# Pooling k and v in the load for six of eight batches, with the schedule laid out anew for it

## The chip, the cores and the metric

The kernel runs on one core of a Trainium2 chip. The metric is the time of one execution on the device, in microseconds (us). Before the change the median of three runs is 214.1 us (213.88 to 214.9).

The engines have short names here as in the profile: PE multiplies matrices (PEld is its loading of the stationary operand), DVE and ACT work elementwise, POOL (GpSimd) issues the loads and sets up constants, SP issues the stores. Each engine executes its own instructions in order; semaphores order the engines among each other.

## The reference

Two parts, one after the other, over 8 batches of 576 tokens:

```python
# attention: q, k, v are (8 batches, 8 heads, 576, 64)
k_p = k.reshape(B, H, 72, 8, D).mean(axis=3)      # 8 neighbours pooled
v_p = v.reshape(B, H, 72, 8, D).mean(axis=3)
scores = scale * np.matmul(q, k_p.transpose(0, 1, 3, 2))
attn = softmax(scores)
x = np.matmul(attn, v_p)                          # -> (8, 576, 512)
# gated FFN: w_in 512x1024, conv_w 3x1024, w_out 1024x512
h = np.maximum(x @ w_in, 0.0)
conv_out = sum(conv_w[k] * shifted(h, k - 1) for k in range(3))   # along the tokens
gate = 1.0 / (1.0 + np.exp(-conv_out))
out = (h * gate) @ w_out
```

All inputs and the output are float32 in memory; the kernel computes in bfloat16 with float32 sums.

## The kernel before

The work of a batch b runs through these stages (line numbers are those of the profile):

- Loads, all issued by POOL, with a cast to bfloat16 on the way: k into `k_b` (L291 for batch 0, L297 for the others), q into `q_b` (L279), v into `v_b` (L321). Each of these tiles exists twice, for even and odd batches, so a load for batch b+2 waits until batch b's data have been read. A row of `k_b` or `v_b` holds the 8 neighbours to be pooled side by side, 8 x 64 = 512 values; there are 576 such rows for each tensor and batch (96 partitions x 6 for k, 72 x 8 for v).
- Pooling on DVE, by halving three times. For k: `kp1` = left half + right half of the row (L406; L402 in two parts for batch 0), `kp2` of that (L414), `ksum` of that (L419). For v: `vp1` (L453), `vp2` (L459) and `vaug` (L465).
- Transposes on PE: `ksum` (L432, copied out to `kTz` at L438 by DVE or ACT) and q (L477, in three groups, copied out to `qT` at L483).
- Scores on PE (L502) per head, exp on ACT (L514), the product with `vaug` on PE (L534, per tile of 128 tokens, "av"), the softmax's division on DVE (L543, L547, into `xx`), the transpose on PE (L561) and a copy to `xT` (L567, DVE or ACT).
- mm1 on PE (L606; L583 in parts for batch 0) and relu on ACT (L612, L590) into `hT`.
- The convolution, per block of 128 features. Blocks that are listed in `off` multiply the three shifted copies on DVE (L632) or ACT (L630), add them on DVE (L638) and take tanh on ACT (L643); the other blocks do it on PE with diagonal matrices `dw` (L680, tanh at L687). The gate is finished on DVE (L660, L666, into `gT`).
- mm2 on PE for pairs of batches (L706), copied to `osb` (L733, L721) and stored by SP (L738, L726).

The order of all this is not written out. A planner inside the kernel (class `Planner`) is given every step with the engines that can do it, an assumed duration, what it reads and writes, and a priority. It plays the steps through once before anything is emitted: on each engine the step that can start first goes next, ties within 0.02 us going to the lower priority number; it also decides between DVE and ACT where a step may run on either, and which of five PSUM slots (three of two banks, two of one) a step gets. The instructions are then emitted in that order, and on the chip each engine keeps it, whatever the real times are. Loads are steps of POOL in this plan, with an assumed time to land. Where the plan sees PE idle in the first 60 us it puts in matmuls of zeros (L254).

The dictionary `PARAMS` holds the numbers that steer the plan: for each batch the priorities of k pooling and transposes (`k`), of q (`q`), of v pooling (`v`), of the scores (`s`, with `ds` from head to head), of av, of the convolution, of mm2 for each group of output tiles; `ld0` and `ps0` for the loads and scores of batch 0; `off` as above; and `acc`, for each batch how many of the three halvings are left to the load. Before the change `acc` is 0 throughout. The code for other values is there already:

Of the kernel before, what the change touches and what calls it, by code (L numbers as in the profile page):

```python
# [13 lines left out]


PARAMS = {
    "off": [(3, 4, 5, 7), (1, 2, 3, 6, 7), (0, 1, 2, 3, 5, 7), (0, 1, 3, 4, 5, 6, 7), (0, 1, 2, 3, 4, 5, 6, 7), (0, 1,
        2, 3, 5, 6, 7), (0, 1, 2, 3, 4, 5, 6, 7), (0, 1, 2, 3, 4, 5, 7)],
    "acc": [0, 0, 0, 0, 0, 0, 0, 0],
    "ld0": [24.66, 0.21, 24.87, 29.62],  # L20
    "ps0": [-13.48, 7.04, 25.02],
    "k": [-8.55, -8.2, -0.72, -12.54, -4.52, -6.0, -8.43, 3.78],
    "q": [-6.36, -3.15, -9.81, 0.97, -2.95, -1.4, -1.88, -9.39],
    "v": [13.91, 4.49, 21.33, 8.22, 1.58, 4.69, 0.09, 45.0],
    "s": [7.35, -3.51, -9.19, -0.57, -3.02, -1.5, -0.0, -6.38],
    "ds": [3.55, 0.71, 1.7, 0.82, 1.36, 0.51, 0.22, -0.62],
    "av": [3.86, 7.06, 3.44, -6.76, -3.51, 4.03, 3.95, -21.37],
    "conv": [3.75, 4.11, 3.3, 3.75, 6.31, 1.04, -10.08, 10.39],
    "mm2": [22.45, 26.52, 17.23, 19.82, 22.07, 21.94, 16.92, 25.3, 19.34, 26.01, 18.91, 22.24, 14.48, 13.2, 21.88,
        3.71, 17.65, 13.25, 17.78, 18.72],  # L30
}


# [793 lines left out]
```

## Time and profile before

The profiled execution:

| what | value |
|---|---|
| time of the profiled execution | 214.1 us |
| its span in the profile | 212.3 us |
| granted PE clock | 1.00 in every stretch |
| PE matmuls, L606 (mm1) | 448, 61.6 us busy |
| PE matmuls, L706 (mm2, 512 columns) | 263 recorded, 63.8 us busy |
| DVE in all | 427 instructions, 185.9 us |
| of it k and v pooling (L402 to L465) | 51 instructions, 35.4 us |
| ACT in all | 301 instructions, 171.1 us |
| DMA, loads (queue 0) | 15648 packets, 16.26 MB written |
| DMA, stores (queue 1) | 5124 packets, 9.45 MB |
| last load issued | 104.2 us (q of batch 7) |

Span is the time from the first to the last recorded instruction of the core; the execution's own time has some 1.8 us around it. A group of instructions is given by line, engine, operation, output and input, and how often it occurs; then the time in which at least one of them ran, the mean duration of one in ns, and the idle time of the engine just before them with what ended it. Matmuls overlap in their pipeline, so the mean duration of one is more than the distance from one to the next.

### The profile page before, as it was taken

The numbers are of one execution on the slowest core, as the hardware profiler recorded it, in microseconds if no ns is written. First come the engines' busy times: TensorE is split into PE (matmuls) and PEld (weight loads), VectorE is DVE, ScalarE is ACT, GpSimd is POOL, SyncE is SP. The second block draws the span as 40 slices with busy tenths as digits, with TensorE's granted clock in tenths as the row PEclk, the third lists the DMA queues.
The fourth block names the chain that finished last, engine by engine and source line by source line (L and its number), as shares of the span: only waits on it lengthen the run. The fifth ranks groups of instructions, "written<-read, shape, count | busy, mean of one in ns | idle before, by whom it ended". The sixth has DMA issues, their size and how long they took to land.

```text
span 212.3 us, 4744 instructions
## 1 busy us (share of the span) xinstructions
PE 200.2 (94%) x1888; PEld 143.7 (68%) x1905; DVE 185.9 (88%) x427; ACT 171.1 (81%) x301; POOL 34.7 (16%) x68
## 2 busy tenths in 40 slices
PE   8998999799999999999999999899999999999983
PEld 8987776687676876577865876566675766655432
DVE  1468699999999999999999999999999998999700
ACT  2074589879996998579999899999799999997632
POOL 7947962011211111020100000000000000000000
PEclk9999999999999999999999999999999999999999
DMA  5999999999999996879442200032020203005125
GB/s 79 157 187 203 205 187 213 196 198 204 183 165 233 178 157 148 121 142 221 67 100 100 99 3 0 3 150 81 21 99 0 102 0 148 3 0 196 66 88 198
DMA packets 20794, 26.02 MB, mean 123 GB/s; under 512 B 2444, under 2 KB 15268, under 8 KB 20772
## 3 DMA queue, kind: packets, MB, share of 16 engines
q0 software_dynamic: 15648, 16.26, 49.6%
q1 hardware_dynamic: 5124, 9.45, 11.9%
q8 instruction: 15, 0.25, 0.5%
q14 instruction: 7, 0.06, 0.1%
HBM read 32.52 MB, written 9.44 MB: 198 GB/s over the span
## 4 chain that ended last, share of the span: by engine, by line
DVE 51%; PE 28%; ACT 3%; issue 3%; ACTq 0%
PE psfB L706 14%; DVE cv L638 10%; DVE cv L632 10%; PE psfA L606 9%; DVE xx L547 7%; DVE gT L666 5%; DVE tg L660 3%; DVE qT L483 3%; DVE vp L453 3%; DVE kp L406 2%; DVE kTz L438 1%; DVE vp L459 1%; PE psfA L502 1%; DVE xT L567 1%; DVE rr L543 1%
## 5 line engine op out<-in xcount | busy, mean ns | idle before, releaser
L706 PE MATMUL psfB<-w_out,gT 128*128 128x512 bf16 (+1 forms) x279 | 65.7, 373 | 2.1 <-ACT osb L733 0.8
L606 PE MATMUL psfA<-xT,w_in 128*128 128x288 bf16 x448 | 61.6, 286 | 0.7 <-ACT hT L612 0.5
L606 PEld LDWEIGHTS <-w_in 128*128 128x128 bf16 x448 | 43.2, 98 | 12.6 <-issue 1.2
L706 PEld LDWEIGHTS <-gT 128*128 128x128 bf16 x296 | 28.1, 98 | 29.4 <-issue 2.1
L638 DVE TENSOR_TENSOR cv<-cv 128x1152 bf16<-128x1152 bf16 (+1 forms) x60 | 40.2, 669 | 0.1
L632 DVE TENSOR_SCALAR cv<-hT,cw 128x576 bf16<-128x576 bf16 x118 | 38.6, 366 | 1.8 <-ACT hT L590 1.1
L514 ACT ACTIVATE attnT<-psfA 72x576 bf16<-72x576 f32 (+3 forms) x70 | 38.4, 604 | 0.3
L612 ACT ACTIVATE hT<-psfA 128x576 bf16<-128x576 f32 x56 | 35.8, 652 | 3.1 <-PE psfA L606 2.9
L643 ACT ACTIVATE tg<-cv 128x1152 bf16<-128x1152 bf16 (+1 forms) x30 | 31.3, 1043 | 5.1 <-DVE cv L638 4.8
L630 ACT ACTIVATE cv<-hT,cw 128x576 bf16<-128x576 bf16 x38 | 28.9, 781 | 0.4
L547 DVE TENSOR_TENSOR xx<-psfA,rr 128x512 bf16<-128x512 f32 x40 | 26.5, 684 | 0.1
L733 ACT COPY osb<-psfB 128x512 f32<-128x512 f32 x32 | 18.5, 583 | 9.6 <-PE psfB L706 6.8
L666 DVE TENSOR_TENSOR gT<-tg,hT 128x1152 bf16<-128x1152 bf16 x32 | 24.0, 750 | 0.2
L502 PE MATMUL psfA<-qT,kTz 128*72 128x288 bf16 (+3 forms) x140 | 23.4, 269 | 0.3
L502 PEld LDWEIGHTS <-kTz 128*72 128x72 bf16 x160 | 16.1, 113 | 4.5 <-issue 1.0
L561 PEld LDWEIGHTS <-xx 128*128 128x128 bf16 x160 | 10.4, 97 | 8.8 <-DVE xx L547 6.1
L660 DVE TENSOR_SCALAR tg<-tg 128x1152 bf16<-128x1152 bf16 x32 | 14.4, 451 | 2.1 <-ACT tg L687 1.1
L534 PE MATMUL psfA<-vaug,attnT 72*128 72x65 bf16 x320 | 14.7, 194 | 1.2 <-ACT hT L590 0.6
L534 PEld LDWEIGHTS <-attnT 72*128 72x128 bf16 x320 | 12.9, 98 | 2.4 <-ACT attnT L514 0.9
L254 PEld LDWEIGHTS <-zero 128*128 128x128 bf16 x192 | 13.4, 109 | 1.0 <-DVE zero L341 1.0
L561 PE MATMUL psbB<-perm,xx 128*128 128x128 bf16 x120 | 11.7, 220 | 1.8 <-DVE xx L547 1.5
L254 PE MATMUL pswA<-zero 128*128 128x128 bf16 x160 | 12.0, 244 | 1.0 <-DVE zero L341 1.0
(65 smaller groups left out, 211.4 us busy)
## 6 DMA issues: line engine op xcount, KB each, us to landing
out_dram<-osb SPq DMA_DIRECT2D x15, 512.0 KB, 2.8
k_b<-in_k_dram POOLq DMA_DIRECT2D x7, 576.0 KB, 11.9
q_b<-in_q_dram POOLq DMA_DIRECT2D x7, 576.0 KB, 11.2
v_b<-in_v_dram POOLq DMA_DIRECT2D x7, 576.0 KB, 10.8
out_dram<-osb SPq DMA_DIRECT2D x5, 256.0 KB, 2.1
w_in<-in_moe_w_in_dram POOLq DMA_DIRECT2D x4, 256.0 KB, 10.3
w_out<-in_moe_w_out_dram POOLq DMA_DIRECT2D x2, 512.0 KB, 17.1
k_b<-in_k_dram POOLq DMA_DIRECT2D x2, 288.0 KB, 4.8
```

The lines of the kernel that those rows point to most:

```text
L502: nc.tensor.matmul(out=t[:, par, :], lhsT=kTz[m][:, par, h * Sp:(h + 1) * Sp], rhs=qT[m][:, 2 * c0:2 * c1, h * A:(h + 1) * A], start=True, ...
L514: nc.scalar.activation(out=attnT[m][:, h, :].rearrange("p (c i x) -> p i c x", i=2, x=32)[:, :, c0:c1, :], in_=view().rearrange("p i (c x) ...
L534: nc.tensor.matmul(out=a[:, h // 4, c:c + D + 1], lhsT=attnT[m][:, h, u0:u0 + 128], rhs=vaug[m][:, h, :], start=True, stop=True)
L547: nc.vector.tensor_tensor(out=xx[i3].rearrange("p (g h e) -> p g h e", g=2, h=4), in0=av_view()[:, :, :, 0:D], in1=rr[i3].rearrange("p (g ...
L606: nc.tensor.matmul(out=t[:, i, 0:HC], lhsT=w_in[:, c, f * P:(f + 1) * P], rhs=xT[m][:, c, i * HC:(i + 1) * HC], start=(c == 0), stop=(c == ...
L612: nc.scalar.activation(out=hT[m][:, f, 2:S + 2].rearrange("p (i x) -> p i x", i=2), in_=slot(key)[:, :, 0:HC], func=ACT.Relu, scale=0.5)
L630: nc.scalar.activation(out=cv[y][:, kk, z, :], in_=src, func=ACT.Copy, scale=s)
L632: nc.vector.tensor_scalar(out=cv[y][:, kk, z, :], in0=src, scalar1=s, scalar2=None, op0=OP.mult)
L638: nc.vector.tensor_tensor(out=cv[y][:, 1, 0:n, :], in0=cv[y][:, 1, 0:n, :], in1=cv[y][:, kk, 0:n, :], op=OP.add)
L643: nc.scalar.activation(out=tg[i3][:, f0 % 2:f0 % 2 + n, :], in_=cv[y][:, 1, 0:n, :], func=ACT.Tanh, scale=0.5)
L666: nc.vector.tensor_tensor(out=gT[(b // 2) % 2][:, fs[0]:fs[0] + 2, o:o + S], in0=tg[i3], in1=hT[m][:, fs[0]:fs[0] + 2, 2:S + 2], op=OP.mult)
L706: nc.tensor.matmul(out=a[:, 0, 0:cols.stop - cols.start], lhsT=g[:, c, t * P:(t + 1) * P], rhs=w_out[:, c, cols], start=(c == 0), stop=(c ...
```

## The change

Only `PARAMS` changes:

```diff
-    "off": [(3, 4, 5, 7), (1, 2, 3, 6, 7), ... (0, 1, 2, 3, 4, 5, 7)],
-    "acc": [0, 0, 0, 0, 0, 0, 0, 0],
-    "ld0": [24.66, 0.21, 24.87, 29.62],
-    "ps0": [-13.48, 7.04, 25.02],
-    "k": [-8.55, -8.2, -0.72, -12.54, -4.52, -6.0, -8.43, 3.78],
-    "q": [-6.36, -3.15, -9.81, 0.97, -2.95, -1.4, -1.88, -9.39],
-    "v": [13.91, 4.49, 21.33, 8.22, 1.58, 4.69, 0.09, 45.0],
-    "s": [7.35, -3.51, -9.19, -0.57, -3.02, -1.5, -0.0, -6.38],
...
+    "off": [(3, 4, 6, 7), (1, 2, 3, 6, 7), ... (0, 1, 2, 3, 4, 5, 6)],
+    "acc": [0, 0, 1, 1, 2, 2, 2, 2],
+    "ld0": [12.84, 6.71, 2.4, 13.31],
+    "ps0": [4.03, 25.62, 23.84],
+    "k": [-1.85, -9.12, 6.44, -3.93, -3.45, -1.33, -20.69, 4.21],
+    "q": [1.98, -27.92, -7.96, -2.38, -0.51, -6.81, -1.77, -5.87],
+    "v": [0.33, -18.28, 26.25, 0.55, 0.78, 4.94, 13.58, 25.95],
+    "s": [-13.2, -14.96, 5.26, -2.65, -3.09, -0.39, -0.96, -3.9],
...
```

`ds`, `av`, `conv` and `mm2` get new numbers in the same way. In `off` only batch 0 (block 6 in place of 5) and batch 7 (block 6 in place of 7) differ.

`acc` leads to code that did not run before. For a batch with `acc` = 1 the load of k is split in two, each bringing half of the 512 values of a row: the first writes the half row, the second adds its half to what is there (L307). With `acc` = 2 there are four loads of a quarter row. v is treated in the same way:

```python
n = 2 ** PARAMS["acc"][b]
w = 512 // n
for i in range(n):
    kw = {} if i == 0 else {"accum_op": OP.add}
    nc.gpsimd.dma_start(out=dst[:, :, 0:w], in_=src[:, :, i * w:(i + 1) * w], **kw)
```

Each adding load reads and writes what the one before it wrote, so POOL issues it only after the one before it has landed. For `acc` = 1 the steps `kp1` and `vp1` on DVE fall away, for `acc` = 2 also `kp2` and `vp2`; the next step reads `k_b` or `v_b` directly, so the tile stays in use until then.

The new priorities give new orders on all engines. In POOL's order the loads now stand as follows, from the first load for batch 2 on (k4.1 is the second load of batch 4's k, and so on):

```
k2.0 q2 v2.0 k3.0 q3 v3.0 k2.1 q4 v2.1 k3.1 q5 v3.1
k4.0 q6 v4.0 k5.0 k4.1 v5.0 v4.1 k5.1 q7
k4.2 v5.1 v4.2 k5.2 k4.3 v5.2 v4.3 k5.3
k6.0 v5.3 v6.0 k6.1 k7.0 v6.1 v7.0 k6.2 k7.1 v6.2 v7.1 k6.3 k7.2 v6.3 v7.2 k7.3 v7.3
```

Of these k6.0 waits for `ksum` of batch 4, v6.0 and v7.0 for `vaug` of batches 4 and 5, k7.0 for `ksum` of batch 5, q6 and q7 for the q transposes of batches 4 and 5. On PE the k transposes of batches 2 to 5 stand later than before among the other matmuls, those of batches 2 and 3 after the whole mm1 of batch 1.

## The prediction

> **What bounds the kernel now.** I read the page's engine shares and slices first, then a table of busy time by stage, then the chain of waits in order of time, then the DMA part.
>
> ```profile
> span 212.3 us, 4744 instructions
> PE 200.2 (94%) x1888; PEld 143.7 (68%) x1905; DVE 185.9 (88%) x427; ACT 171.1 (81%) x301; POOL 34.7 (16%) x68
> DMA  5999999999999996879442200032020203005125
> ```
>
> PE, DVE and ACT are all nearly full, and DMA is full for the first 80 us and nearly empty after 115 us. The stages tell more (window, its length, then busy us and instructions of each engine):
>
> ```profile
> 0.00:46.00 46.00, 41.89 (x531) 35.52 (x532) 33.40 (x77) 27.21 (x67) 26.91 (x57) 1.00 1.17 180
> 46.00:78.00 32.00, 30.98 (x301) 23.09 (x302) 31.45 (x69) 29.63 (x51) 4.68 (x7) 1.00 1.10 194
> 78.00:119.00 41.00, 39.47 (x365) 27.28 (x368) 40.91 (x96) 34.83 (x60) 3.15 (x5) 1.00 0.62 119
> 119.00:155.00 36.00, 35.04 (x319) 24.75 (x321) 36.00 (x85) 34.12 (x55) 0.00 (x0) 1.00 0.14 53
> 155.00:212.30 57.30, 52.77 (x386) 33.02 (x388) 44.14 (x105) 45.33 (x72) 0.00 (x0) 1.00 0.22 83
> ```
>
> From 46 to 155 us DVE never rests (108.4 of 109 us) and the chain of waits runs over DVE in most of this stretch; from 157 us it runs over PE. But PE is idle only 1.02 + 1.53 + 0.96 = 3.5 us between 46 and 155. Busy time of pipelined matmuls covers short gaps, so I also count by spacing, which the chain gives where PE runs without a break:
>
> ```profile
> 162.94 1.73 PE psfB L706 x8
> 171.30 0.52 PE psfA L534 x16
> 177.32 5.88 PE psfA L606 x48
> ```
>
> That is 216 ns for 512 columns, 33 ns for 65 and 122 ns for 288; the 128-column transposes stand 56 ns apart, the 96-column ones 42. The PE stream, priced so, needs 102.7 us from the q transposes of batch 2 (L477, start 46.7 us) to the k transposes of batch 7 (L432, start 155.3 us), which took 108.6: 5.9 us of PE gaps. So a faster DVE can win 3.5 to 5.9 us there and no more.
>
> **The change, part by part.** Pooling taken off DVE:
>
> ```profile
> L453 DVE TENSOR_TENSOR vp<-v_b 72x2048 bf16<-72x2048 bf16 x7 | 8.5, 1215 | 0.0
> L406 DVE TENSOR_TENSOR kp<-k_b 96x1536 bf16<-96x1536 bf16 x7 | 6.7, 962 | 0.8 <-DMA k_b<-in_k_dram 0.8
> L459 DVE TENSOR_TENSOR vp<-vp 72x1024 bf16<-72x1024 bf16 x7 | 4.8, 680 | 0.0
> L414 DVE TENSOR_TENSOR kp<-kp 96x768 bf16<-96x768 bf16 x8 | 4.4, 547 | 0.0
> ```
>
> L406 and L453 go for six batches, L414 and L459 for four: 6 x (0.962 + 1.215) + 4 x (0.547 + 0.680) = 18.0 us. The new order also moves work between DVE and ACT: DVE takes one kTz copy (0.45), one qT copy (0.42), seven whole and two half xT copies (7 x 0.417 + 2 x 0.286) and two osb copies (2 x 0.686), 5.7 us, and gives seven products (L632, 0.366) to ACT, -2.6. DVE: -18.0 + 5.7 - 2.6 = -14.9 us. ACT gives up 7.3 us for these copies and takes 7 x 0.781 = 5.5: -1.8 us. On PE the matmuls are the same but for three warm-up ones (0.17 us); the lists "off" change in which filters they hold, not in how many (52 before and after), so this edit costs nothing. Worth on the path: of the 3.5 to 5.9 us of gaps, ACT (near 9/10 full) and the order keep some; I take **-3**, bounds 0 and -5.9. After 155 us nothing is taken: there PE, not DVE, sets the end.
>
> Reordering of batch 0's loads: the same two k loads go first; q then stands behind the identity (0.22 + 0.29 us) and w_in starts about 0.3 us later than 7.97. DVE waits 1.0 us in all for those first k loads and 1.6 for v. I take 0, bounds -1 and +1.
>
> Loads: a pooled load reads 1/2 (batches 2, 3) or 1/4 (4 to 7) of each row and adds it to the destination, and each waits for the one before it to land. For k and for v alike the nine issues of before (two halves of batch 0, one each of batches 1 to 7) become 2 + 1 + 2 x 2 + 4 x 4 = 23, so 28 more in all. While POOL stands in such a wait, all loads behind it in its order wait too, q included. On POOL each costs what these do, 0.74 to 0.87 us: 22 us, on an engine that is 84% idle; nothing. What counts is the DMA queue itself, which works in order:
>
> ```profile
> q0 software_dynamic: 15648, 16.26, 49.6%
> k_b<-in_k_dram POOLq DMA_DIRECT2D x7, 576.0 KB, 11.9
> v_b<-in_v_dram POOLq DMA_DIRECT2D x7, 576.0 KB, 10.8
> ```
>
> A k or v load is 576 packets whatever its width. Single packets in the trace took 98 ns at 1024 B written (k, v before) and 60 ns at 512 B (w_in). A line through both gives 41 ns at 256 B, so an unaccumulated quarter load keeps 16 engines 576 x 41 / 16 = 1.48 us; four of them are 5.9 us against 3.5 us for the one load they replace. The trace has no accumulating packet. It reads 512 B of source and 256 B of destination; by bytes read (512 B at 41 ns, 1024 B at 60) that is 50.5 ns, 1.82 us a load. Lower bound 41 ns; upper bound two packets' worth, 82 ns, 2.95 us. I take 50.5, nearest to the two rows. Batches 2 and 3 (60 ns x 2 x 576 against 98 x 576) add 0.8 us each to a queue that is full until 80 us, but their pooled sums stand late in the new order (below), so I price them at nothing; without that cover it would be 3.2 us.
>
> Where does it become late? I placed the changed streams on the clock by the spacing count plus the lag of count behind clock that the kernel before shows (12.4 us at its batch-4 k transposes, 13.6 at batch 5, 14.4 at batch 6, 15.1 at the q transposes of batch 6). Batch 2's and 3's k sums then stand at 62 and 66 us, more than 10 us behind their loads. But POOL's issue of q for batch 7 waits for the last six q transposes of batch 5 (count 65.9, so 78.5 us), and behind it in POOL's order stand 20 quarter loads up to the last one of batch 6's k. The sum that needs it (ksum, L419) and the six transposes behind it on PE stand at count 104.3, so 119.4 us. Between: 41 us. Work for the DMA engines in it: q7, 128 packets x 361 ns / 16 = 2.9 us; 4 first and 16 accumulating loads, 5.9 + 16 x 1.82 = 35.0; some 4.5 output stores of 256 packets x 85 ns / 16, 6.1; 1.8 us from issue to first packet and from last packet to semaphore (1.5 us seen). Sum 45.8: **4.8 us late**. At 41 ns it is 40.3, just in time; at 82 ns 63.9, 23 us late. These sums let all 16 engines work alike; a v load took 5.3 us from first to last packet for 3.6 us of mean engine time, so the ten v loads can be half as long again: 10 x 1.75 x 0.5 = 8.7 at most. I add a third of it, **+2.9**. Behind the late sum wait DVE (products of batch 4) and, in order, PE (mm1 and mm2), so the wait is paid by both.
>
> A rule of the Trainium skill speaks against the change more strongly: SBUF — State Buffer, in "SBUF: two separate sides", says that DVE's two-port modes lock GpSimd out while it writes the descriptors of its DMAs, and gives 620 ns growing to 3100. The row disagrees: POOL's k and v issues took 740 to 798 and 752 to 869 ns with DVE 40.9/41 busy, and 704 to 822 at 1.3 us with DVE idle. By the rule a chain of four would be some 10 us longer; by the row, nothing.
> DMA: Bandwidth & Descriptors (Specifications) says that transfers below 512 B lose line rate to a read-modify-write; no run here shows packets of 256 B on this queue, and it would push toward the upper bound.
>
> Sum: 212.3 - 3 + 0 + 4.8 + 2.9 = 217.0 span; the profiled execution took 214.1, 1.8 more than its span, and the median of the runs is 214.1 too, so **218.8 us**.
>
> **Rivals.**
> 1. Loads in time (slack I do not see, or packets at 41 ns): only the relief counts, 212.3 - 3 + 1.8 = 211.1; with all gaps won 208.2. For it: 41 ns gives 40.3 us for 41. Against: it leaves no idle time in a queue where each load waits for another. Chance 0.31.
> 2. Relief and lateness cancel: at 41 ns the queue is 40.3 + 2.9 - 41 = 2.2 us late and 3 us are won, 213.3, which with a packet a little dearer is 214.1 within 0.5%. Chance 0.08.
> 3. Forecast, on the slower side: accumulating packets at 45 to 60 ns. The DMA queue between q of batch 7 and the k sum of batch 6 is the place; it decides from some 44 ns on, and gives 215.6 at 45 ns and 224.3 at 60. For it: three quarters of a packet's reading at 60 ns is certain to take more than half of it. Against: none was seen. Chance 0.41.
> 4. Accumulating packets cost two packets or more: late 22.9 us, 212.3 - 3 + 22.9 + 1.8 = 234; the k sums of batches 4 and 5 are then late as well. For it: an extra read of its own; against: 9.6 ns for 256 B more read is what the two rows' slope gives. Chance 0.20.
>
> **How the numbers follow.** Point: case 3, 218.8. The range leaves out half of case 4 and the best tenth of case 1: 209.5 to 231; case 3 alone is 215.6 to 224.3. A half per cent, 1.1 us, is what a measurement can tell here (the three runs span 213.88 to 214.9). Faster 0.31, same 0.08, slower 0.61.
>
> **What would show it.** Right: DVE waiting on the DMA of k_b or v_b at L419 and L465 for several us around 95 to 130 us, PE idle in the same slices at L432, DMA slices at 9 from 80 to 130 us, packets of 256 B near 50 ns. DVE busy near 171 us either way. Wrong: no such waits and a PE gap total below 3 us in the middle; or waits at batch 2 or 3, which I priced at nothing; or POOL issues that grow to several us, as the rule has it.

## The result, and the profile after

The changed kernel takes 225.75 us (median; 225.47 to 226.49) against 213.99 us before on the same chip: a ratio of 1.0556, 95% interval [1.0503, 1.0609]. The forecast was 218.8 us. Its direction held; the kernel lost 11.8 us where the sum gave 4.7, so the size was off by more than half. The profiled execution took 225.47 us, its span is 223.5.

The page of the kernel after, its lines for span, engines, granted clock and DMA:

```profile
span 223.5 us, 4771 instructions
PE 203.8 (91%) x1894; PEld 144.7 (65%) x1908; DVE 177.6 (79%) x413; ACT 171.6 (77%) x295; POOL 75.6 (34%) x99
PEclk9999999999999999999999959999999999999999
DMA  5999999979999789997999995201201102102325
```

DVE's busy time fell by 8.3 us, and it was idle for 45.9 us where it had been idle for 26.4. DMA is nearly full to slice 24 (134 us), not to 80 us. One PEclk slice, the 24th, shows 5. The same kernel by stage (window, length, then busy us and count of PE, PEld, DVE, ACT, POOL, granted clock, DMA share, GB/s):

```profile
46.00:78.00 32.00, 29.86 (x280) 20.53 (x280) 26.21 (x59) 24.99 (x41) 13.08 (x13) 1.00 1.03 151
78.00:119.00 41.00, 39.30 (x352) 27.04 (x355) 38.37 (x90) 37.12 (x59) 24.09 (x21) 1.00 1.14 123
119.00:155.00 36.00, 28.87 (x252) 20.90 (x253) 27.07 (x64) 25.42 (x43) 9.33 (x7) 0.91 0.62 72
120.00:130.00 10.00, 3.18 (x35) 2.41 (x34) 3.12 (x6) 3.87 (x8) 5.71 (x5) 0.87 1.20 122
130.00:140.00 10.00, 9.89 (x91) 7.45 (x93) 8.21 (x21) 6.71 (x12) 2.62 (x2) 0.79 0.71 50
```

Two stretches lose. From 120 to 130 us PE worked 3.2 of 10 us: one large wait. From 46 to 78 us PE made 280 matmuls where it had made 301, with DVE idle for 5.8 us: a loss without a large gap. The waits of the kernel after name the first (who waits for whom: us in all, times, longest):

```profile
PEld L432 <- DVE ksum L419: 8.7, 4, 7.1
DVE ksum L419 <- DMA k_b<-in_k_dram: 6.8, 1, 6.8
POOL v_b L307 <- DMA v_b<-in_v_dram: 13.0, 7, 3.7
POOL k_b L307 <- DMA k_b<-in_k_dram: 6.6, 5, 2.3
```

And its chain of waits from 110 to 130 us (start, duration, what):

```profile
110.05 6.99 DMA v_b<-in_v_dram
117.03 0.29 issue
117.33 2.31 POOL v_b L307 x2
119.64 9.68 DMA k_b<-in_k_dram
...
129.34 0.57 DVE ksum L419
```

This is the place that the prediction named: the k sum of batch 6 (L419) stands at 129.3 us for its last adding load, which itself was issued late, since POOL waited for an adding v load to land. PE's transposes (L432) wait behind it for 7.1 us.

To see the loss without a gap, each matmul's start is set against the time that PE's stream up to it needs at the spacings of the prediction (the count). The table gives start minus count, in us; what it grows by is PE time lost. A step at one place is a wait; a slow rise over many matmuls is a loss without a large gap. The last three rows are experiments that follow.

| count, us | 33 | 50 | 70 | 104 | 107 | 138 | 189 |
|---|---|---|---|---|---|---|---|
| before | 10.7 | 11.6 | 12.5 | 15.2 | 15.2 | 16.6 | 18.9 |
| after | 10.9 | 10.8 | 15.9 | 18.6 | 27.7 | 28.1 | 30.0 |
| new order, first loads only | 11.0 | 11.0 | 16.1 | 17.4 | 17.5 | 17.9 | 19.8 |
| old order, first loads only | 11.2 | 11.8 | 12.2 | 13.5 | 13.5 | 14.5 | 16.3 |
| new order, batch 2 planned early | 10.9 | 11.9 | 13.2 | 15.3 | 16.1 | 17.0 | 18.8 |

After loses 5.1 us between counts 50 and 70, where before loses 0.9, and 9.1 us between 104 and 107.

### The profile page after: what moved, and what is told of

Its sections match the earlier page's. It is cut to its first block, busy times and chain, and to the rows that moved or that the text cites. A ratio compares the mean times of both kernels' runs of the same rounds, so it can differ in the third digit from the quotient of the medians.

```text
span 223.5 us, 4771 instructions
## 1 busy us (share of the span) xinstructions
PE 203.8 (91%) x1894; PEld 144.7 (65%) x1908; DVE 177.6 (79%) x413; ACT 171.6 (77%) x295; POOL 75.6 (34%) x99
## 4 chain that ended last, share of the span: by engine, by line
PE 56%; DVE 15%; ACT 13%; DMA 7%; POOL 4%; issue 3%; another core or an unknown queue 1%; POOLq 0%; DVEq 0%
PE psfB L706 18%; PE psfA L606 17%; ACT attnT L514 7%; PE pswA L254 4%; DMA k_b<-in_k_dram 4%; DVE cv L632 4%; DVE cv L638 4%; DMA v_b<-in_v_dram 3%; PE psfA L502 3%; DVE xx L547 3%; PE psfA L680 2%; PE psbB L561 2%; POOL v_b L307 2%; PE psfA L534 2%; PE psbB L477 2%
## 5 line engine op out<-in xcount | busy, mean ns | idle before, releaser
L606 PE MATMUL psfA<-xT,w_in 128*128 128x288 bf16 x448 | 59.6, 286 | 0.1
L606 PEld LDWEIGHTS <-w_in 128*128 128x128 bf16 x448 | 43.3, 98 | 11.8 <-issue 0.5
L632 DVE TENSOR_SCALAR cv<-hT,cw 128x576 bf16<-128x576 bf16 x111 | 37.7, 380 | 3.7 <-ACT hT L590 1.9
L514 ACT ACTIVATE attnT<-psfA 72x576 bf16<-72x576 f32 (+3 forms) x70 | 37.4, 595 | 2.8 <-PE psfA L502 2.6
L630 ACT ACTIVATE cv<-hT,cw 128x576 bf16<-128x576 bf16 x45 | 33.9, 775 | 0.6
L307 POOL DMA_DIRECT2D v_b<-in_v_dram x20 | 26.5, 1443 | 20.8 <-DMA v_b<-in_v_dram 13.0
L307 POOL DMA_DIRECT2D k_b<-in_k_dram x20 | 26.9, 1427 | 12.7 <-DMA k_b<-in_k_dram 6.6
L733 ACT COPY osb<-psfB 128x512 f32<-128x512 f32 x30 | 17.2, 579 | 10.8 <-PE psfB L706 8.4
L502 PE MATMUL psfA<-qT,kTz 128*72 128x288 bf16 (+3 forms) x140 | 23.9, 275 | 1.6 <-ACT attnT L514 0.6
L660 DVE TENSOR_SCALAR tg<-tg 128x1152 bf16<-128x1152 bf16 x32 | 14.9, 467 | 1.9 <-ACT tg L687 1.0
L561 PEld LDWEIGHTS <-xx 128*128 128x128 bf16 x160 | 10.2, 98 | 8.5 <-DVE xx L547 5.8
L534 PE MATMUL psfA<-vaug,attnT 72*128 72x65 bf16 x320 | 14.5, 194 | 0.7 <-ACT hT L590 0.5
L687 ACT ACTIVATE tg<-psfA 128x576 bf16<-128x576 f32 x12 | 7.8, 650 | 8.2 <-PE psfA L680 8.1
```

Of the source, the lines that this page charges most:

```text
L307: nc.gpsimd.dma_start(out=dst[:, :, 0:w], in_=src[:, :, i * w:(i + 1) * w], **kw)
L502: nc.tensor.matmul(out=t[:, par, :], lhsT=kTz[m][:, par, h * Sp:(h + 1) * Sp], rhs=qT[m][:, 2 * c0:2 * c1, h * A:(h + 1) * A], start=True, ...
L514: nc.scalar.activation(out=attnT[m][:, h, :].rearrange("p (c i x) -> p i c x", i=2, x=32)[:, :, c0:c1, :], in_=view().rearrange("p i (c x) ...
L606: nc.tensor.matmul(out=t[:, i, 0:HC], lhsT=w_in[:, c, f * P:(f + 1) * P], rhs=xT[m][:, c, i * HC:(i + 1) * HC], start=(c == 0), stop=(c == ...
L630: nc.scalar.activation(out=cv[y][:, kk, z, :], in_=src, func=ACT.Copy, scale=s)
L632: nc.vector.tensor_scalar(out=cv[y][:, kk, z, :], in0=src, scalar1=s, scalar2=None, op0=OP.mult)
```

## Experiments

The kernel before was run again beside each group of experiments and took 213.3 to 213.7 us (median; single executions 212.8 to 215.8). Each ratio is to the runs of its own group, with the 95% interval in brackets; the quoted texts are what was expected before each run.

### What the relief, the order and the loads cost, one at a time

The new order, all adding loads left out:

```diff
 for i in range(n):
-    kw = {} if i == 0 else {"accum_op": OP.add}
+    if i:
+        return
+    kw = {}
```

> The changed kernel with every adding load left out (only the first half or quarter of each k and v row is loaded for batches 2 to 7, so pooling is incomplete); all engines keep the changed kernel's order. Theory 'queue' (the additions fill the DMA engines and make k of batch 6 late): the 6.8 us wait of DVE at ksum L419 and the half-clock stretch vanish, about 225.8 - 7.1 - 1.9 = 216.8 us, with the 3 us lost near the scores of batch 2 still there. Rival 'order' (the new order loses the time by itself): 224 to 226. Rival 'loads throughout' (the loss near batch 2 comes from the loads too): about 213 or below.

214.94 us, 1.0065 [1.0046, 1.0084]. The large wait is gone, and still the kernel is no faster than before. The table's third row grows by 5.1 us between counts 50 and 70, as after does, though nothing is added there and neither DVE nor PE waits for a load of batch 2 or later: this loss is not made by late data.

The same loads in full, none of them adding (`kw = {}` throughout, so each overwrites the one before it):

> The changed kernel with the same halves and quarters loaded, one after the other with the same waits, but each overwriting instead of adding (so only the last part of each row is pooled). Theory 'queue': packets 41 ns instead of 56, and 16 adding loads on the way to batch 6's last k quarter become 16 x 0.54 = 8.6 us shorter, which takes the wait of 6.8 us away: about 217 us. Rival 'chain' (what counts is that each load waits for the one before it, not the packets' length): the wait stays, above 222 us. Rival 'issue' (POOL's 1.43 us per adding issue against 0.75 is the limit): DMA engines would show idle time between the loads in the changed kernel, and this run would be faster with packets still near 56 ns.

217.27 us, 1.0164 [1.0096, 1.0232]; the profiled execution, 215.44 us, has a span of 213.5 and no wait of the k sum. Its runs spread from 215.44 to 218.41. By the medians, 8.5 of the 10.8 us between the kernel with the first loads only and the change belong to the adding, that is to longer packets and longer issues together, and not to the number of loads or to each waiting for the one before it. The queue shows it: the two lines are queue 0 (packets, MB, share of 16 engines), the kernel after from 84 to 112 us, then this one from 80 to 108 us.

```profile
q0 software_dynamic: 8819, 2.44, 102.4%
```

```profile
q0 software_dynamic: 8138, 2.30, 79.2%
```

Single packets of 256 B written took 41 ns plain and 56 adding, packets of 512 B 60 and 84. POOL's issues differ as well (busy us, mean ns of one | idle before), after and then this kernel (20 loads, of which 14 add in the kernel after):

```profile
L307 POOL DMA_DIRECT2D k_b<-in_k_dram x20 | 26.9, 1427 | 12.7 <-DMA k_b<-in_k_dram 6.6
```

```profile
L307 POOL DMA_DIRECT2D k_b<-in_k_dram x20 | 15.5, 774 | 22.3 <-DMA k_b<-in_k_dram 11.9
```

Had the longer issues alone been the limit, the DMA engines of the kernel after would have stood idle between the loads, and from 84 to 112 us they hardly did. So the longer packets are the likelier limit; what the longer issues add to it is not shown.

To price the relief without the new order, the first half (batches 2 and 3) or quarter (4 to 7) alone is loaded in the order of before, and DVE's first sums are left out:

```diff
+HALF = (2, 3, 4, 5, 6, 7)
...
+if b in HALF:
+    w = 128 if b > 3 else 256
+    nc.gpsimd.dma_start(out=k_b[m][:, :, 0:w], in_=rows_k(b)[:, :, 0:w])
+    return
```

> The kernel before, in its own order on every engine, with the pooling stages that the change saves left out of DVE's stream (kp1, vp1 for batches 2 to 7, kp2, vp2 for 4 to 7, 18.0 us) and only the first half or quarter of each of these rows loaded (pooling is incomplete). It prices the relief by itself. Theory of the prediction: 3 us of the 3.5 to 5.9 us of PE gaps come back, about 210.5 us. Rival 'the relief is worth nothing' (PE's gaps are ACT's and the order's): 213 or more, as the run with the new order and no adding loads (214.9) might suggest. If 'new order costs 3 us' holds, this run stands about 3 to 4 us below that one.

215.46 us, 1.007 [1.0036, 1.0103]. This kernel had the loads of batch b+2 ahead of the last sum of batch b in program order, since that sum now reads `k_b` itself: the sum took the later batch's rows and waited for them (5.0 us once). Its time does not answer the question. With the loads held back until that sum:

> As x9, but without its flaw: there some loads for batch b+2 stood ahead of the pooled sum of batch b that still reads the tile, so that sum waited for loads of a later batch. Here POOL issues such a load only after that sum; the order on PE, DVE and ACT is the old one, less the 18.0 us of pooling, and only the first half or quarter of the rows of batches 2 to 7 is loaded (pooling is incomplete). Theory 'relief is worth 3 us': 210 to 211.5 us. Rival 'relief is worth nothing, PE's gaps are not DVE's': 213 to 214.5.

216.09 us, 1.0062 [1.0021, 1.0103]. PE lost 2.3 us less than before up to count 104, and then 4.6 us at q of batch 7: its load stood in POOL's order behind a v load that waited for its buffer. With q ahead of it:

```diff
-while queue and need.get(queue[0][3].name) in done | {None}:
...
+held = held or need.get(x[3].name) not in done | {None}
+if not held or x[3].name.startswith("ldq"):
```

> The order of the kernel before, with the relief of VectorE alone: batches 2 and 3 load one half of the rows of k and v, batches 4 to 7 one quarter, and nothing is added to them, so the pooling leaves out the other rows; q is issued ahead of a v load that still waits for its buffer. Theory A (the relief by itself shortens the kernel by some 2.5 to 3 us, and the loss near the scores of batch 2 belongs to the new order of the work): 210 to 212 us, and TensorE's wait for q of batch 7 (4.6 us with q behind v) is gone; then the run with the new order and the first quarters alone (214.9 us) puts the price of the new order at about 3 us. Rival B (the relief is worth nothing, since VectorE's idle time only moves): 213 to 214.5 us. Rival C (short loads in this order make another wait late): over 215 us, and the waits name it.

210.62 us, 0.9851 [0.9805, 0.9897]: by the medians (210.62 against 213.37) the relief alone is worth 2.75 us; the interval allows 2.2 to 4.2. Part of it may come from the shorter loads rather than from DVE. The new order with the same loads is 4.3 us slower than this.

### Why the new order costs

PE's timeline (start, us, instructions, idle before in brackets) at the scores of batch 2, first in the kernel with the new order and the first loads only, then in the one with the old order:

```profile
64.24 0.94 PE L504 MATMUL psfA<-qT,kTz 128*72 128x288 bf16 x4 [0.16 <-ACT attnT L516]
65.38 0.94 PE L504 MATMUL psfA<-qT,kTz 128*72 128x288 bf16 x4 [0.20 <-ACT attnT L516]
66.52 0.94 PE L504 MATMUL psfA<-qT,kTz 128*72 128x288 bf16 x4 [0.20 <-ACT attnT L516]
```

```profile
50.64 0.65 PE L523 MATMUL psfA<-qT,kTz 128*72 128x288 bf16 x4
51.13 1.89 PE L727 MATMUL psfB<-w_out,gT 128*128 128x512 bf16 x7
52.86 0.66 PE L523 MATMUL psfA<-qT,kTz 128*72 128x288 bf16 x4
53.35 0.91 PE L701 MATMUL psfA<-hT,dw 128*128 128x288 bf16 x6
```

Four scores every 1.14 us, where their spacing needs 4 x 0.122 = 0.49: they go at the pace of exp on ACT, which frees their slots (two of some 0.57 us). PE looks busy, with idle stretches of 0.2 us; only the distance from start to start shows the loss. In the old order mm1, mm2 and the convolution stand between the scores and fill it. By the count, 2.8 of the 5.1 us are lost from the k transposes of batch 2 to the last of these scores (61.3 to 67.7 us) and the rest behind them, up to 78 us.

Moving the k sum, transposes and scores of batch 2 forward by hand, in the changed kernel:

```diff
+put = {
+    "qTe.3.2": ["kp2.2", "ksum.2"],
+    "oe.0.0": ["kT.2", "kz.2.0", "kz.2.1"],
+    "mm2.0.1.0": ["sc.2.7.0"],
...
```

> The changed kernel with one change of order: pooled sum and transposes of batch 2's k and five of its eight score steps are put between the mm2 tiles of batch pair 0 that stood ahead of them (same instructions). Theory 'scores without cover': PE's 3 us at the scores of batch 2 (waiting for exp on ACT, 0.57 us a head) shrink by 1.5 to 2.5 us, and as the loads behind are released earlier by as much, the time falls to about 223.5. Rival (the loss there is due to the late loads of batch 2): k of batch 2 is not there earlier, DVE waits at kp2 L414 and the time stays at 225.8 or rises.

226.41 us, 1.0606 [1.0549, 1.0662]: nothing gained. PE now waited 1.2 us for `kTz`, 0.8 for `osb` and twice 0.5 for exp in the same stretch; the loss only took other forms (six matmuls of zeros that stood ahead of the q transposes of batch 4 also fell away, 0.3 us). DVE had no wait for a load there, so the rival's reason does not show either. This neither confirms nor refutes the pace of exp as the cause.

The planner books an adding load at 1.3 times its bytes. In the kernel with the first loads only, telling it that batch 2's second half is free, with k's old number, has the plan itself put these scores earlier, among mm1 and mm2:

```diff
-nbytes=int(H * S * D * 4 / n * 1.3)
+nbytes=(0 if i and b == 2 else int(H * S * D * 4 / n * 1.3))
...
-"k": [-1.85, -9.12, 6.44, ...
+"k": [-1.85, -9.12, -0.72, ...
```

> The run with the first quarters alone, planned differently in one batch: the planner is told that batch 2's second half costs nothing on the queue, and k of batch 2 has its number of before (-0.72), so that its sum, transposes and scores are planned earlier; 14 of its 16 scores then lie among matmuls of mm1 and mm2 in twos and fours, where the new order has them behind mm2 with 14 of 16 back to back. As in that run, only the first half or quarter of the rows of batches 2 to 7 is loaded, so pooling is incomplete. Theory A (the new order's price of some 4 us, 214.9 against 210.6 us, is the scores of batch 2 without other TensorE work between them, which comes from the planner taking batch 2's k as late by the adding load): the time without TensorE's work grows by 1 us or less between matmul counts 50 and 70 (4.9 with the new order) and the time is 211 to 212.5 us. Rival B (the loss is elsewhere in the new order, in its other numbers): 214 to 215.5 us, the growth only moved.

213.63 us, 0.9982 [0.9949, 1.0015], between the two theories. The growth from count 50 to 70 fell from 5.1 to 1.3 us (last row of the table), as theory A has it; but 2.5 us of the 2.9 gained at count 70 were kept up to 100, and only 1.0 to the end, lost again near counts 104 and 107 and beyond. So the packed scores are shown as the place of the first loss, and planning them earlier was worth 1.3 us of the 4.3 for the whole. The planner laid out the rest anew as well, so these 1.3 us are those of the new plan and not of the scores alone; where the other numbers lose the rest is not settled.

### The wait and what follows it

To see what the lower clock behind the wait costs, 112 matmuls of zeros fill it, ahead of the k transposes of batch 6:

```diff
+if b == 6:
...
+    for _ in range(112):
+        nc.tensor.matmul(out=w, lhsT=zero[:, 0:P], rhs=zero[:, 0:P], start=True, stop=True)
```

> The changed kernel with 112 more matmuls of zeros (6.2 us at 55 ns) ahead of the k transposes of batch 6, where PE stands idle for 7 us. Theory 'queue': the wait itself stays, but the granted clock stays at 1.00 and the 1.9 us that PE loses after the wait come back: about 224 us. Rival 'no clock loss' (the 1.9 us are something else): 225.5 or more.

225.14 us, 1.0539 [1.05, 1.0578]: the clock stayed up (0.997 against 0.984 in the mean), and 0.6 us came back. In the changed kernel 1.8 us are lost just behind the wait (counts 104.6 to 107); with the zeros nothing is lost there, but 2.4 us further on, up to count 138, where the changed kernel loses 0.4. So the loss behind the wait mostly moved.

Halves in place of quarters for batches 6 and 7, new numbers (`"acc": [0, 0, 1, 1, 2, 2, 1, 1]`, replanned):

> The changed kernel with acc 1 instead of 2 for batches 6 and 7: 8 half loads in place of 16 quarters (60 + 84 = 144 ns a row instead of 41 + 3 x 56 = 209, 5.2 us of the DMA engines a tensor instead of 7.5), four DVE additions more (2.5 us); the planner lays it out anew. Theory 'queue': some 9 us less DMA work ahead of batch 6's k, the wait there falls from 6.8 us to 0 to 2: 217 to 220 us. Rival 'latency of the chain': the wait shrinks too, but DMA engines then show idle time ahead of it. Rival 'neither': 224 or more.

222.32 us, 1.035 [1.0279, 1.042]: 3.4 us of the loss are gone, with the longest wait of the k transposes for their sum down from 7.1 to 2.0 us. That is less than the 217 to 220 us expected: shortening the wait by 5 us won 3.4.

### Adding loads in the old order

The old numbers with the new `acc`, and with `acc` 1 for batches 6 and 7 alone, both replanned:

> The kernel before with nothing but the list acc of the change; the planner lays out a new order from the old priorities. Theory 'queue': the same 24 adding quarter loads stand in the same window, the DMA engines are full from some 75 us and a pooled sum of batch 5, 6 or 7 waits several us: 218 to 232 us. Rival 'the new numbers are at fault, not the loads': 214 or below.

> The kernel before with acc 1 for batches 6 and 7 alone; the planner lays out a new order from the old priorities, putting other loads between the halves. A candidate for a version that beats both: 4.4 us of DVE gone, 4 x 1.7 = 6.8 us more DMA work where the engines are a quarter busy. Theory: no late load; with relief worth a little, 212.5 to 214; if a priority falls badly in the new order, up to 218. Above 220 would mean that adding loads cost something that I do not see.

234.99 us, 1.0945 [1.0877, 1.1013], and 214.77 us, 1.0031 [0.9996, 1.0066]. In the first, DVE and PE wait little for k and v directly (the k sum 1.1 us) and PE's loss is spread over many small waits, but the chain of waits runs over adding v loads and POOL's waits for them from 64 to 120 us. It is slower than the 232 us at most that were expected, and old numbers under the new loads are no neutral reference for the order. The second shows no difference from before, and misses the gain that was hoped for.

The old order kept, with two halves for batches 2 to 7, and for 5 to 7:

```diff
+nc.gpsimd.dma_start(out=k_b[m][:, :, 0:256], in_=rows_k(b)[:, :, 0:256])
+nc.gpsimd.dma_start(out=k_b[m][:, :, 0:256], in_=rows_k(b)[:, :, 256:512], accum_op=OP.add)
```

> The kernel before, in its own order, with k and v of batches 2 to 7 loaded as two halves, the second adding, and kp1 and vp1 of these batches gone from DVE (13.1 us). Theory 'queue': a pair of halves keeps the DMA engines 576 x (60 + 84) / 16 = 5.2 us against 3.5, 12 times, which the queue has room for after 80 us but hardly before; k and v of batches 2 and 3 may come 1 to 3 us late, the later ones not: 211 to 214 us. Rival 'adding loads are always too late': above 217.

> As the run before, but with halves for batches 5, 6 and 7 alone, whose loads fall where the DMA engines have room; kp1 and vp1 of three batches gone (6.5 us of DVE). Theory: no late loads, PE gaps shrink by a third to a half of what the full relief gives: 212 to 213 us. Rival 'relief is worth nothing': 213.3 to 214.

290.62 us, 1.3566 [1.35, 1.3631], and 237.57 us, 1.1096 [1.1051, 1.114]. Both have the order of load and sum described above, so a sum reads the later batch's rows and DVE waits for them, up to 41 us in the first and 27 in the second; their times do not answer the question. With the loads held back, batches 5 to 7:

> As x4b with the same flaw mended: old order, k and v of batches 5, 6 and 7 as two halves, the second adding right behind the first in POOL's order. The DMA engines have room there (5.2 us a pair against 3.5), so theory 'queue' alone expects 212 to 214 us. Rival 'POOL's own order' (each adding load holds POOL for the 6 to 11 us until the first half has landed, and with it q and the loads of the next batch): q or k of batches 6 and 7 late, 216 us or more.

225.81 us, 1.0518 [1.0458, 1.0578]. Its waits:

```profile
POOL v_b L328 <- DMA v_b<-in_v_dram: 27.7, 3, 11.6
POOL k_b L300 <- DMA k_b<-in_k_dram: 23.7, 3, 9.7
PEld L492 <- DMA q_b<-in_q_dram: 9.9, 2, 9.3
```

The second half stands directly behind the first, POOL waits 8 to 9 us in the mean for each landing, and q, issued behind that, comes late by 9.3 us. The same loads with others between the two halves, in POOL's order `k5.0 q5 v5.0 k5.1 k6.0 v5.1 q6 k6.1 v6.0 k7.0 v6.1 k7.1 q7 v7.0 v7.1`:

> The order of the kernel before; batches 5, 6 and 7 of k and v are loaded as two halves, the second added to the first, and other loads stand between the two halves in GpSimd's order, so that its wait for the landing of the first half is short. VectorE loses the first sums of three batches (6 sums). Theory A (adding loads cost only where they come late or where GpSimd stands in their wait): 212 to 213.3 us, no wait for k, v or q on TensorE or VectorE above 1 us. Rival B (at 56 to 84 ns for each adding packet the last batch is late again): above 215 us, with a wait for k or v of batch 6 or 7. Rival C (relief this late in the kernel is worth nothing): 213.3 to 214.5 us.

212.97 us, 0.9968 [0.9938, 0.9998]: 12.8 us for nothing but the order of the issues. Its waits cannot be read, since its profile is of an execution that took 409.79 us for a reason that it does not show; the other eleven took 212.15 to 214.57. One batch more, and two:

> The old order with two halves in batches 4 to 7, other loads between the two halves in GpSimd's order: one batch more than the run with batches 5 to 7. Theory A (one more batch of VectorE relief brings about 0.5 us while its loads are in time): 211.8 to 212.8 us. Rival B (the queue is full up to about 80 us in the kernel before, and batch 4's adding half makes the loads behind it late): 214 to 217 us, with a wait for k, q or v of batches 4 to 6.

> The old order with two halves in batches 3 to 7, one batch more than the run that took 211.7 us. Theory A (each batch more of VectorE's relief brings 0.5 us or more while loads are in time): 210.5 to 211.5 us. Rival B (the queue is full from the start to about 80 us, and batch 3's adding halves push the loads behind them past their use): 213 to 218 us, with waits of TensorE or VectorE for k, q or v of batches 4 to 6 that the run with four batches does not have.

211.71 us, 0.9881 [0.9827, 0.9936], with halves from batch 4 on: 1.2% faster than before, and faster than the change. In its profile PE has no wait for a load, and DVE's longest is 1.1 us, so the late q of the run with back-to-back halves is gone. From batch 3 on it is 213.04 us, 0.9955 [0.9921, 0.999]; there POOL stood 22.9 us in waits for v landings and 22.6 for k, up to 13.5 at a time (12.7 and 3.7 with four batches), and DVE's second k sum waited up to 2.0 us for a load. Of three, four and five batches in this order, four came out best. The page of the kernel with four:

```profile
PE 201.0 (95%) x1888; PEld 145.0 (69%) x1905; DVE 179.8 (85%) x419; ACT 170.7 (81%) x301; POOL 46.2 (22%) x76
DMA  5999999999899999979662760030120203004125
```

DMA goes idle only after 127 us (slice 25 on), and PE is at 95%.

## Why the prediction was right or wrong

- Relief: predicted -3, measured -2.75 (210.62 against 213.37 us). The reading that PE's gaps bound it, and not the DVE time that falls away, was right. That the size came so close is partly luck: -3 was chosen between 0 and -5.9, not worked out. DVE's own time was off: the sum gave -14.9 us and 171 us busy, and the kernel after has 8.3 us less, 177.6 busy. The forecast did not rest on it.
- Order: this is the step that failed. The sum has only two terms for the new order, both 0: the loads of batch 0, and those of batches 2 and 3 ("their pooled sums stand late in the new order, so I price them at nothing"). For the order of the matmuls it has none, and the relief's bound of 0 says that relief and order together cannot lose. With the first loads only, where nothing is added, they lose: 214.94 us against 213.31 before, +1.6 in place of -3, and 4.3 us more than the same loads in the old order (210.62). The two zeros themselves hold roughly: no wait of DVE for k or v of batches 2 and 3 shows in the kernel after, though a pair of halves cost 60 + 84 = 144 ns a row against the 120 assumed. What was missed is that with that sum the scores behind it were late too, and stood nearly alone, without the mm1, mm2 and convolution that run between them in the old order. The experiments show this place, 2.8 us by the count; a plan with these scores earlier won 1.3 us in the total, and what makes up the rest of the 4.3 stays open.
- Lateness: predicted +4.8 + 2.9 = 7.7; the k sum of batch 6 waited 6.8 us, PE's load of it 7.1. The place, batch and line were right; the wait at L465 that was also named does not show. From q of batch 7's issue (82.4 us, predicted 78.5) to that sum are 46.9 us; the sum had 48.7. Inside it sizes were off in opposite directions, so that 6.8 against 7.7 is luck in part: an adding packet took 56 ns, not 50.5 (16 loads x 576 packets x 5.5 ns / 16 engines = 3.2 us more), and the 2.9 us for uneven engines were not needed: the loads alone filled 102.4% of all 16 engines from 84 to 112 us. A share over 100%, to which the stores added 12.2%, also says that packet times overlap, so that the sum of loads and stores one after the other counts some time twice.
- What stands around the wait was left out. Against the kernel with the first loads only, after loses 1.2 us before count 104 to smaller waits, 7.2 at the wait, and 1.8 from there to count 107, 10.2 in all, as the spans have it (223.5 - 213.3). The prediction's 7.7 is 2.5 short. Of the 1.8 us behind the wait, holding the clock up with zeros brought back only 0.6 in the total.
- POOL at "nothing": an adding load's issue is in the chain of waits (2.31 us for two issues at 117 us), so it is part of the 46.9 us, and the mean issue of k took 1427 ns (single ones up to 3.2 us), not 740 to 870. Issues that grow were named as a sign of being wrong; as the queue was full meanwhile, what they cost by themselves is not shown. That a load behind an adding one waits with it was told in the prediction but not priced; in the pair of orders above it made 12.8 us.
- The sum: -3 + 0 + 7.7 = 4.7 predicted; -2.75 + 4.3 + 10.8 = 12.4 by the medians, against 11.8 for the change itself (the kernel before differs by 0.6 us between the two groups of runs). Of the 7.7 between 4.7 and 12.4, 4.3 are the order, some 3 what surrounds the wait, and 0.3 the relief.
- The rule on DVE locking GpSimd out, in the Trainium skill's SBUF — State Buffer ("SBUF: two separate sides"): plain quarter loads took 774 ns in the mean with DVE at 83%, so the row still disagrees; the longer issues came with the adding, not with DVE. The prediction's own row was read too widely: of its issues only three, of 740 to 839 ns, lie in the stretch with DVE busy for 40.9 of 41 us. And the page ties the lock to DVE's two-port modes, and the trace does not tell which mode DVE ran in; two v issues that lay wholly under scalar products of DVE (L660, L632; 47.4 and 55.8 us) took 842 ns. On the rule of DMA: Bandwidth & Descriptors (Specifications) about transfers below 512 B: plain packets of 256 B written (512 B read) took the 41 ns of the line through the larger ones, so no extra step shows at that size on this queue; packets with both sides below 512 B were not run.

## What to carry to other kernels

Work taken off an engine is worth the gaps that it leaves on the engine that sets the end, and a new order can cost more than that: look for matmuls that go at another engine's pace, by their distance from start to start, not by idle time. In this kernel an adding load was best issued when the one before it had landed anyway, with other loads between them (212.97 against 225.81 us), since POOL stands still in its wait and holds back all the loads that follow. When something is hidden because its user is late, ask what else that user's lateness uncovers.

## What the runs showed of the hardware

Adding packets took 56 ns at 256 B written and 84 at 512 B, plain ones 41 and 60, so adding ones about 1.4 times as much. POOL's issues of the pooled k loads, of which 14 in 20 add, took 1.43 us in the mean against 0.77 for the same loads without adding; the last four adding issues of the kernel after, which stood apart, took 1.25 to 1.40. From 127.4 to 134.2 us, beginning in the last part of PE's wait of 7 us, the granted PE clock was at half (0.79 in the mean from 130 to 140 us), and filling that wait with matmuls of zeros brought back only 0.6 us.
